# Softmax attention with a rational feed-forward part on one core: seven-token key descriptors, four-token value descriptors, score tiles by parity, scalars loaded later

## The chip, the cores and the metric

The kernel runs on one core of one Trainium2 chip. The metric is the device time of one execution in microseconds (us), the median over several executions. Every ratio compares with the kernel before on the same chip, in alternating rounds. All executions that this study quotes were classed as fast by the measuring program, so no slow run is mixed in.

The engines are TensorE (PE in the listings; PEld is its weight loading), VectorE (DVE), ScalarE (ACT), GpSimd (POOL) and SyncE (SP). GpSimd issues most loads from DRAM into SBUF, the on-chip memory. PSUM is the small memory into which TensorE writes its results. "L540" is a line of the kernel. The same statement has another line number in the kernel before and after, for example the first linear layer is L539 before and L540 after. The "ramp" is the first part of an execution, up to about 43 us, in which TensorE still waits for data and for other engines.

## The reference

There are 8 batches, 12 heads, 448 tokens and 64 numbers a head. The attention has one more term in its denominator. Its result goes through a linear layer (768 to 2048), a rational function of each element, and a second linear layer (2048 to 768).

```python
scores = scale * np.matmul(q, k.transpose(0, 1, 3, 2))
m = np.max(scores, axis=-1, keepdims=True)
e = np.exp(scores - m)
attn = e / (np.sum(e, axis=-1, keepdims=True) + np.exp(-m) + 1e-09)
x = np.matmul(attn, v)                    # then (batch*tokens, heads*64)
h = x @ w_in
P = a[0] + a[1]*h + a[2]*h**2 + a[3]*h**3
Q = 1.0 + abs(b[0])*abs(h) + abs(b[1])*h**2
out = (P / (Q + 1e-06)) @ w_out
```

The exponential may be taken without the maximum, since e / (sum of e + exp(-m)) is exp(score) / (sum of exp(score) + 1). That is what the kernel does.

## The kernel before

The kernel is written as steps with an estimated duration, an engine and what they depend on. A small planner walks over them when the program is built and fixes the **order** of the instructions on each engine. On the chip each engine runs its instructions in that order and waits for its operands. The planner takes written landing times of the loads, a price for a change of TensorE's tiling mode (`switch`), a further reluctance to change it, and a patience:

```python
    def order(self, switch, reluctance, patience, calm):
        ...
                for eng in cost:
                    t = max(self.free[eng], r)
                    k = key
                    if eng == "PE" and m != mode:
                        k += reluctance[self.free["PE"] > calm]
                    ahead[eng].append((t, k, s))
        ...
    plan.order(0.095, (0.05, 0.8), 1e-09, 25)
```

A head has 448 tokens, so each of 64 partitions holds seven consecutive tokens. The kernel before loads them as three, three and one. A descriptor is one such run, 768 bytes in DRAM for three tokens and 256 for one. (The loads narrow to 16 bits on the way, and the trace counts half of these bytes.) NS is 3, NT is 7, and a "quad" is one of the three groups of four heads.

```python
    def three(src, b, half):
        return src[b].rearrange("h (p j) d -> p h (j d)", j=NT)[
            :, :, NS * half * D:NS * (half + 1) * D]

    def load_rest(src, b, dsts, eng=nc.gpsimd):
        of = src[b].rearrange("h (p j) d -> p h j d", j=NT)
        for half, dst in enumerate(dsts):
            eng.dma_start(out=dst, in_=of[:, H // 2 * half:H // 2 * (half + 1), NT - 1, :])

    def load_k(b, part):
        ...
        if part < 3:
            for half in range(2):
                nc.gpsimd.dma_start(
                    out=k4[rows(half), 4 * part * w:4 * (part + 1) * w].rearrange(
                        "p (t x) -> p t x", x=w),
                    in_=of_quad(three(k, b, half), part))
        ...
        if part >= 3:
            load_rest(k, b, [...])
```

The first batches are then worked on as follows. Keys and queries are turned by TensorE (`tk`, `tq`). A score tile (`sps`) is four 64x64 matmuls. ScalarE takes its exponential (`e`, 128x896). TensorE forms the denominators (`den`, 16 matmuls) and the products with the values (`u`, two times 16). ScalarE makes the reciprocal of the denominator with a logarithm and an exponential (`rden`), and VectorE multiplies (`xt`). When all six parts of `xt` of a batch and a quarter of w_in are there, the first linear layer (`hp`, six matmuls a step) can run.

```python
        nc.scalar.activation(out=e[:, :, 0:n], in_=sps[:, :, 0:n], func=AF.Exp, scale=scale)
...
    def inverse(b, z, qd, step, eng):
        if eng == "ACT" and step == 0:
            nc.scalar.activation(out=r, in_=dens.pop((b, z, qd))[:, 0:w],
                                 func=AF.Ln, bias=one_c)
        elif eng == "ACT":
            nc.scalar.activation(out=r, in_=r, func=AF.Exp, scale=-1.0)
...
    def gemm1(b, z, fcs):
        ...
                nc.tensor.matmul(
                    out=hp[:, n * w:(n + 1) * w],
                    lhsT=w_in_sb[:, c, fc * 128:(fc + 1) * 128],
                    rhs=xt[:, c, queries(b, z)], start=(c == 0), stop=(c == NDC - 1),
                )
```

Nine matmuls on zeros (`busy_work(9)`, tile `idle`) stand at the head of TensorE's work, while the first data are on their way.

## Time and profile before

| what | value |
|---|---|
| time, three runs | 427.45 us median (427.42 to 428.1) |
| span of the profiled run | 426.0 us |
| TensorE busy | 414.5 us |
| first matmul of the first layer | 31.69 us |
| 25th matmul of the first layer, after which TensorE is nearly full | 42.56 us |

The profile's page begins with the busy time of each engine and its share of the span. Further down it lists the DMA queues: packets, megabytes, and the time of those packets as a share of all 16 DMA engines.

```profile
PE 414.5 (97%) x3693; PEld 208.6 (49%) x3693; DVE 332.0 (78%) x493; ACT 309.1 (73%) x361; POOL 113.4 (27%) x176
...
q0 software_dynamic: 55936, 22.50, 44.3%
```

The list of TensorE's waits has these lines (who waited, for what, us in total, times, longest).

```profile
PE sps L460 <- ACT e L472: 2.1, 4, 1.0
PE hp L539 <- DVE xt L524: 1.3, 1, 1.3
...
PE hp L539 <- DMA w_in_sb<-in_moe_w_in_dram: 0.6, 1, 0.6
```

TensorE waits for w_in, at 31.69 us, for 0.6 us. It waits 1.3 us at 42.56 us for a product of VectorE.

### The profile page before, as it was taken

To read this page: it belongs to the slowest core of one execution; us is meant where nothing else is said; L and a number is where in the kernel's file an instruction comes from. 1 tells how busy PE (TensorE), PEld (TensorE's weight loads), DVE (VectorE), ACT (ScalarE), POOL (GpSimd) and SP (SyncE) were. 2 spreads that over 40 slices of the span, in tenths; PEclk is the share of its full clock that TensorE was granted. 3 is DMA by queue.
4 is the path that set the end of the run, shared out by engine and by line. 5 is a ranking of instruction groups with operands and counts; after the bars stand their busy time and mean duration, and the time that the engine had idled before them with its cause. 6 is when DMAs were issued, how large, how long until landed. Compare 5 with 4: busy or idle time off the path is not lost.

```text
span 426.0 us, 8968 instructions
## 1 busy us (share of the span) xinstructions
PE 414.5 (97%) x3693; PEld 208.6 (49%) x3693; DVE 332.0 (78%) x493; ACT 309.1 (73%) x361; POOL 113.4 (27%) x176
## 2 busy tenths in 40 slices
PE   7798999999999999999999999999999999999996
PEld 3443444444554455544554455444455545556664
DVE  4446899999959995999729994139999799899721
ACT  5898887998828993498946997699998396465300
POOL 8875405542720801540008001020002000004100
PEclk9999999999999999999999999999999999999999
DMA  9999999999799999990299814970001102002223
GB/s 140 171 157 197 166 207 155 157 196 209 127 188 213 112 150 195 141 159 2 51 209 128 100 57 96 177 103 2 2 1 57 37 2 57 18 2 75 75 74 75
DMA packets 116025, 47.28 MB, mean 111 GB/s; under 512 B 90256, under 2 KB 115984, under 8 KB 115984
## 3 DMA queue, kind: packets, MB, share of 16 engines
q0 software_dynamic: 55936, 22.50, 44.3%
q1 hardware_dynamic: 59824, 24.06, 25.2%
q8 instruction: 29, 0.48, 0.5%
q10 hardware_dynamic: 224, 0.15, 0.1%
q14 instruction: 12, 0.10, 0.1%
HBM read 45.62 MB, written 11.01 MB: 133 GB/s over the span
## 4 chain that ended last, share of the span: by engine, by line
PE 76%; ACT 8%; DVE 6%; POOL 3%; DMA 3%; issue 1%; POOLq 0%; ACTq 0%
PE op L634 31%; PE hp L539 29%; PE sps L460 7%; PE u L480 6%; ACT e L472 4%; PE den L480 3%; ACT c L593 2%; DMA w_in_sb<-in_moe_w_in_dram 2%; DVE c L581 1%; DMA q<-in_q_dram 1%; POOL k L193 1%; DVE g L591 1%; DVE w L586 1%; DVE xt L524 1%; ACT g L136 1%
## 5 line engine op out<-in xcount | busy, mean ns | idle before, releaser
L539 PE MATMUL hp<-xt,w_in_sb 128*128 128x448 f16 x768 | 154.4, 353 | 1.8 <-DVE xt L524 1.3
L472 ACT ACTIVATE e<-sps 128x896 f16<-128x896 f32 x168 | 146.3, 927 | 9.1 <-PE sps L460 6.9
L634 PE MATMUL op<-w_out_sb,g 128*128 128x384 f16 x768 | 130.4, 326 | 0.1
L539 PEld LDWEIGHTS <-w_in_sb 128*128 128x128 f16 x768 | 71.6, 98 | 76.6 <-issue 13.3
L634 PEld LDWEIGHTS <-g 128*128 128x128 f16 x768 | 73.3, 98 | 54.7 <-issue 7.7
L604 POOL COPY gx<-g 128x256 f16<-128x256 f16 x32 | 23.0, 740 | 216.0 <-DVE g L591 110.2
L586 DVE TENSOR_TENSOR w<-w,g 128x1792 f16<-128x1792 f16 (+1 forms) x66 | 69.7, 1056 | 0.3
L593 ACT ACTIVATE c<-c,oneeps_c 128x1792 f16<-128x1792 f16 (+1 forms) x33 | 57.8, 1751 | 12.9 <-DVE c L581 12.9
L138 DVE CAST g<-hp 128x448 f16<-128x448 f32 x78 | 48.1, 618 | 15.7 <-PE hp L539 15.3
L460 PE MATMUL sps<-qT,kT 64*64 64x448 f16 x672 | 53.5, 365 | 3.1 <-ACT e L472 2.1
L136 ACT ACTIVATE g<-hp 128x448 f16<-128x448 f32 x50 | 27.2, 546 | 38.8 <-PE hp L539 38.7
L595 ACT ACTIVATE c<-c 128x1792 f16<-128x1792 f16 (+1 forms) x33 | 54.8, 1660 | 0.2
L524 DVE TENSOR_TENSOR xt<-u,rden 128x448 f16<-128x448 f32 x48 | 27.9, 615 | 30.6 <-ACT rden L504 29.8
L588 DVE TENSOR_SCALAR w<-w,abc 128x1792 f16<-128x1792 f16 (+1 forms) x66 | 44.8, 679 | 0.4
L136 ACT ACTIVATE osb<-op 128x384 f32<-128x384 f32 (+1 forms) x25 | 12.2, 489 | 42.8 <-DVE osb L138 23.1
L480 PE MATMUL u<-e,v 128*32 128x448 f16 x768 | 40.7, 353 | 0.0
L138 DVE COPY osb<-op 128x384 f32<-128x384 f32 (+2 forms) x33 | 17.8, 539 | 26.0 <-PE op L634 25.9
L591 DVE TENSOR_TENSOR g<-w,c 128x1792 f16<-128x1792 f16 (+1 forms) x33 | 34.8, 1054 | 1.1 <-ACT c L595 0.7
L581 DVE TENSOR_TENSOR c<-c,w 128x1792 f16<-128x1792 f16 (+1 forms) x33 | 34.8, 1054 | 0.3
L460 PEld LDWEIGHTS <-kT 64*64 64x64 f16 x672 | 15.4, 104 | 38.1 <-issue 35.8
L480 PEld LDWEIGHTS <-v 128*32 128x32 f16 x768 | 20.4, 97 | 15.6 <-issue 0.6
L583 DVE TENSOR_SCALAR w<-g,abc 128x1792 f16<-128x1792 f16 (+1 forms) x33 | 24.2, 734 | 0.4
(49 smaller groups left out, 266.4 us busy)
## 6 DMA issues: line engine op xcount, KB each, us to landing
q<-in_q_dram POOLq DMA_DIRECT2D x23, 224.0 KB, 6.0
v<-in_v_dram POOLq DMA_DIRECT2D x14, 288.0 KB, 5.6
k<-in_k_dram POOLq DMA_DIRECT2D x12, 288.0 KB, 6.8
w_in_sb<-in_moe_w_in_dram POOLq DMA_DIRECT2D x16, 192.0 KB, 7.8
w_out_sb<-in_moe_w_out_dram POOLq DMA_DIRECT2D x4, 768.0 KB, 9.3
out_dram<-osb SPq DMA_DIRECT2D x16, 168.0 KB, 2.3
out_dram<-osb SPq DMA_DIRECT2D x16, 144.0 KB, 1.9
out_dram<-osb SPq DMA_DIRECT2D x16, 120.0 KB, 1.8
```

What stands on the lines that cost most here:

```text
L136: nc.scalar.activation(out=out, in_=src, func=AF.Copy)
L138: nc.vector.tensor_copy(out=out, in_=src)
L460: nc.tensor.matmul(out=sps[rows(c), bank, m * w:(m + 1) * w], lhsT=kT[rows(half), key:key + 64], rhs=qT[rows(half), o:o + w], start=True, ...
L472: nc.scalar.activation(out=e[:, :, 0:n], in_=sps[:, :, 0:n], func=AF.Exp, scale=scale)
L480: nc.tensor.matmul(out=dst[32 * t:32 * t + 32], lhsT=lhs(t, n), rhs=ets[b, z, qd, i][:, bank, m * w:(m + 1) * w], start=(n == 0), stop=(n ...
L539: nc.tensor.matmul(out=hp[:, n * w:(n + 1) * w], lhsT=w_in_sb[:, c, fc * 128:(fc + 1) * 128], rhs=xt[:, c, queries(b, z)], start=(c == 0), ...
L581: nc.vector.tensor_tensor(out=c, in0=c, in1=m, op=ALU.mult)
L586: nc.vector.tensor_tensor(out=m, in0=m, in1=h, op=ALU.mult)
L588: nc.vector.tensor_scalar(out=m, in0=m, scalar1=a1 if step == 5 else a0, scalar2=None, op0=ALU.add)
L593: nc.scalar.activation(out=c, in_=c, func=AF.Ln, bias=oneeps_c)
L595: nc.scalar.activation(out=c, in_=c, func=AF.Exp, scale=-1.0)
L634: nc.tensor.matmul(out=op[:, 0:wide_of(nh)], lhsT=lhs(fc), rhs=w_out_sb[:, fc, columns(nh)], start=(fc == 0), stop=(fc == NFC - 1),)
```

## The change

The change has six parts, in one diff.

1. Keys come with all **seven tokens in one descriptor**, values with four (or three), so there are fewer descriptors and fewer load instructions.
2. The score tiles pair tokens s and s + 4 and are sorted by head parity (from batch 2 on by the parity of head, quad and token together).
3. The early key load takes whole runs of seven. Keys of the first quad are therefore narrowed to 16 bits and turned in pieces.
4. The two small loads of the scalars a and b are issued later.
5. The order of the loads changes. Three quarters of w_in now stand ahead of the values of batch 1.
6. The written landing times, the planner's parameters and the start keys are new, and there are 18 small filler steps of one matmul on zeros. In the second linear layer the steps of batch 0 are sorted, and output copies of batch 2 no longer go to ScalarE.

```diff
-    def three(src, b, half): ...
-    def load_rest(src, b, dsts, eng=nc.gpsimd): ...
+    def keys_of(b, half, qd=None):
+        some = k[b, H // 2 * half:H // 2 * (half + 1)].rearrange("h (p j) d -> p h (j d)", j=NT)
+        return some if qd is None else some.rearrange("p (t g) x -> g p t x", g=NQ)[qd]
 ...
+        for half in range(2):
+            to = loaded[b, "k"][rows(half)].rearrange("p (h x) -> p h x", x=NT * D)
+            if part < 3:
+                to = to.rearrange("p (t g) x -> g p t x", g=NQ)[part]
+            nc.gpsimd.dma_start(out=to, in_=keys_of(b, half, part if part < 3 else None))
 ...
+        for above, half, n0, n1, heads in classes():          # values: four or three tokens
+            first = above + n0
+            nc.gpsimd.dma_start(
+                out=v4[rows(half), heads].rearrange("p h s d -> p h (s d)")[
+                    :, :, first * D:(first + n1 - n0) * D],
+                in_=of_half(v, b, half, n0, n1, heads))
 ...
-    nc.sync.dma_start(out=abc, in_=moe_a.unsqueeze(0).to_broadcast([128, 4]))
-    nc.sync.dma_start(out=bbc, in_=moe_b.unsqueeze(0).to_broadcast([128, 2]))
+    def load_scalars():
+        for dst, src in ((abc, moe_a), (bbc, moe_b)):
+            nc.vector.memset(dst, 0.0)
+            nc.sync.dma_start(out=dst, in_=src.unsqueeze(0).to_broadcast(dst.shape))
 ...
+        ('k0', 2), ('q0', 1), ('k0', 1), ('q0', 2), ('v0', 4), ('k1', 4),     # first loads
+        ('q1', 0), ('q1', 2), ('q1', 1), ('w', 0), ('w', 1), ('w', 2), ('v1', 4),
 ...
+    for n in range(1, 19):
+        add("warm", ("warm", n), 1000, {"PE": (0.22, 0.22)}, lambda: busy_work(1),
+            deps=[("s", 0, 0, 0, 0)], takes=[("gen", ("warm", n))], mode="full")
 ...
-        for t, eng, name, fn in plan.order(0.095, (0.05, 0.8), 1e-09, 25):
+        for t, eng, name, fn in plan.order(0.095, (0.2, 1.0), 0.3, 60):
```

## The prediction

> **What bounds the kernel now.** I read first the busy time of the engines by stretch (columns: stretch, its length, busy us and instructions of PE, weight loads, DVE, ACT and POOL, the granted clock, DMA share, GB/s).
>
> ```profile
> 0.00:5.00 5.00, 3.80 (x9) 1.19 (x9) 1.86 (x13) 1.28 (x1) 3.82 (x11) 1.00 0.60 122
> 5.00:31.70 26.70, 22.36 (x422) 11.88 (x422) 12.05 (x30) 23.22 (x32) 22.38 (x39) 1.00 1.36 162
> 31.70:43.00 11.30, 9.93 (x107) 4.22 (x108) 6.82 (x11) 9.43 (x12) 6.69 (x11) 1.00 1.41 197
> 43.00:110.00 67.00, 66.69 (x609) 31.25 (x608) 66.03 (x95) 59.20 (x66) 24.32 (x31) 1.00 1.15 177
> ...
> 422.00:426.00 4.00, 0.00 (x0) 0.00 (x0) 0.27 (x1) 0.33 (x1) 0.00 (x0) 0.89 0.25 56
> ```
>
> TensorE is full from 43 us to 422 us: 0.31 us are missing in the first 67 us of it and similarly little later. Of the 11.5 us without TensorE work, 1.2 lie before its first instruction, 4.0 after its last, 4.34 between 5 and 31.7 us (26.70 less 22.36), 1.37 between 31.7 and 43. The last two, 5.7 us or 1.3% of the time, are all that earlier data can give back. Anything more has to come from less TensorE work.
>
> Next the chain that ended last, in order of time, as far as the first matmul of the first linear layer (start, us, what).
>
> ```profile
> 3.92 2.46 POOL k L193 x4
> ...
> 7.18 6.03 DMA q<-in_q_dram
> ...
> 18.30 1.32 POOL k L181 x2
> 19.62 0.71 POOL q L163
> 20.33 1.23 POOL v L211 x2
> 21.56 0.91 POOL w_in_sb L380 x2
> ...
> 23.19 8.37 DMA w_in_sb<-in_moe_w_in_dram
> ...
> 31.69 1.30 PE hp L539 x6
> ```
>
> Until 31.69 us the chain is GpSimd issuing loads one after the other and the first quarter of w_in landing behind them. After that TensorE has big independent matmuls to put between the attention steps, so the start of the first linear layer is the moment at which TensorE becomes full. Last, ScalarE in the same stage (timeline; start, us, instructions, idle before).
>
> ```profile
> 15.89 2.53 ACT L472 ACTIVATE e<-sps 128x896 f16<-128x896 f32 x3
> 20.00 3.35 ACT L472 ACTIVATE e<-sps 128x896 f16<-128x896 f32 x4 [1.57 <-PE u L480]
> ...
> 29.31 0.64 ACT L501 ACTIVATE rden<-den,one_c 128x448 f32<-128x448 f32 x1
> 29.98 0.58 ACT L504 ACTIVATE rden<-rden 128x448 f32<-128x448 f32 x1
> ```
>
> ScalarE is the second limit of the ramp. Its exponentials begin at 7.30 us, take 0.83 us each when they follow one another (five in 4.15), and batch 0 needs 21 of them and three reciprocals of 0.54 + 0.58. The last reciprocal ends at 30.56, the last attention product on DVE near 31.7. So in the kernel before w_in and the attention of batch 0 are ready at practically the same time, and **both** must move for a gain.
>
> **What the skill says.** The page "DMA: Bandwidth & Descriptors", section "Why small descriptors are slow (HBM only)", gives each packet a fixed cost beside its bytes. The trace agrees in direction. From 0 to 28 us, 11365 packets carried 4.62 MB (407 B each); from 40 to 50 us, 2649 packets carried 1.96 MB (740 B each). With 16 engines busy for about 26 and 10 us, a packet took 36.6 and 60.4 ns. A straight line through these two (my estimate from two points) is 7.5 ns a packet and 0.0715 ns a byte. The page "TensorEngine Tiling (Array Packing)", section "Key Properties", says that a change of tiling mode drains TensorE. Here 6 matmuls of the first layer take 1.24 us alone and 18.16/16 = 1.135 us inside a run of 96; 16 of the second take 2.71 alone and 2.60 in a run. So a change of mode costs some **0.1 us**. The page "TensorE: Matmul & The Clock Gate", section "What's actually happening", says that an idle window of about 3.4 us halves the clock. Here the longest wait of TensorE in the ramp is 1.3 us and the granted clock is 1.00 throughout: there is no clock to win.
>
> **The change, part by part.**
>
> *Fewer descriptors and fewer issues.* Keys of a batch go from 1536 runs of three tokens and 768 of one to 768 of seven. By the line above that is 1536 x (7.5 + 27.5) + 768 x (7.5 + 9.2) = 66.6 engine-us before and 768 x (7.5 + 64.1) = 55.0 after, or 4.2 and 3.4 us on 16 engines. Values go from 2304 runs to 1536 of four or three tokens: 4.2 to 3.8 us. Two key batches (a third of one comes by the early loads anyway) and one value batch lie ahead of w_in: about 1.8 us less DMA. GpSimd issues 28 loads before the first of w_in now, and 16 afterwards: 12 x 0.66 us = 7.9 us less issuing, in a stage where it is 22.38/26.70 busy. Issuing and transfer overlap, so the sum doesn't count. Taking 2 to 4 us together, w_in lands at **27.5 to 29.5** instead of 31.55 us. The landing times written into the changed kernel say 28.7 for it against 32.0 in the old one; they order instructions only, but point the same way.
>
> *ScalarE's part of the ramp.* One key load per half, with tokens 0 and 4 narrowed first, should bring the first exponential from 7.3 to about 6.6 us; query and key loads of quads 1 and 2 come earlier, values all at once near 17 us. Then 6.6 + 21 x 0.83 + 3 x 1.12 = 27.4 is the earliest end of the last reciprocal, with two products of 0.58 us 28.6. Allowing for half of the old idle time, the first layer starts at about **29 us** instead of 31.69. The same attention work lies before it: 22.36 us of TensorE, less two score tiles of batch 1 (0.6) and with 0.3 more for the key transposes, which for the first quad go in halves (98 instead of 84, at 0.044 us). So idle time from 5 to 29 us is 24.0 - 22.1 = 1.9 instead of 4.34: **-2.4 us**.
>
> *The gap at 42.6 us* (1.29 us, matmuls waiting for a product that gives back their PSUM buffer) belongs to the old order of work. I give the new order an even chance: **-0.7**.
>
> *Score tiles by parity.* Number, shape and pairing in the array stay: 168 tiles of four 64x64 matmuls, seven to a head quad. No cost: **0**.
>
> *The new order.* The timeline of TensorE shows 212 changes of mode, 166 of them after 43 us; there, 18 stretches of scores are a single tile and 58 a pair. Greater reluctance to change (0.2 and 1.0 instead of 0.05 and 0.8) should pair some of them. Each pairing saves two changes, 0.2 us; four pairings give **-0.8**.
>
> *Scalars later, filler matmuls.* The two scalar loads leave the head of the SyncE queue; their transfers are 1.1% of DMA there: 0. Up to 18 fillers of 0.22 us run only where the plan sees TensorE idle, but each is a change to full mode and takes a PSUM buffer: **+0.2**, though the profile will count up to 4 us of them as busy.
>
> *Stages after 110 us.* DMA is below full there and TensorE full, so cheaper key and value loads buy nothing.
>
> **The rivals.** (1) *A new wait for values of batch 1.* The changed load order puts three quarters of w_in ahead of them, yet the written landing times still have them at 31.8 us, before the second quarter of w_in. Three quarters at 786 KB and 196 GB/s are 4 us each, so after 27.7 + 8.0 + 3.9 they land near 39.6. If TensorE reaches those products in order at 35 to 36 us it stalls for up to 4 us, and scores behind it stall too. For it speaks the inconsistency, against it that someone tuning on the chip would have seen it. A chance of one in four of 2.5 us: **+0.6** in the mean; if it comes, the time is 426.5 to 428. (2) *ScalarE stays the bound of the ramp.* Then w_in lands early for nothing, and only the switches and the earlier start pay: 426 to 427. For it speaks 23.22 of 26.70 us busy; against it the 1.57 us wait, which comes from waiting on values in order. (3) *The new order of the whole kernel also makes TensorE's work shorter*, by pairing nearly all scores and joining runs of the layers: 30 changes fewer are another 3 us, so 421 to 422. Nothing in the profile before speaks for so many.
>
> **Range and chances.** -2.4 - 0.7 - 0.8 + 0.2 + 0.6 = -3.1 us, and I take 0.2 back for instructions that the new plan misplaces elsewhere: 427.45 - 2.9, **about 424.5 us**. Rivals 1 and 2 set the upper end, 428.0, rival 3 and the whole 5.7 us of gaps the lower, 421.0. Faster by over 2% needs under 419.1 us, more than all idle time of the ramp: 4%. Slower by over 2%, above 436 us, would need several stalls of 4 us: 2%. Within 2%: 94%.
>
> **What would show it.** Right: w_in lands at 27.5 to 29.5 us, the first matmul of the first layer starts near 29, idle time of TensorE from 5 to 31.7 us apart from fillers falls below 2.5 us, software queue packets fall from 55936 by 8 x 2304 = 18432 less the part now loaded early, to about 37500, and the score group keeps its 168 x 4 matmuls at some 365 ns. The switches part is shown by under 210 changes of mode, fillers aside. Wrong: a wait of TensorE for values at 35 to 40 us (rival 1); a first exponential not before 7 us or a last reciprocal of batch 0 after 29.5 (rival 2); gaps of TensorE after 43 us of over 1 us in sum; or a clock below 1.00 in the ramp. Should the time fall by over 6 us, my claim that TensorE's work stays the same is what failed.

## The result, and the profile after

| | before | after |
|---|---|---|
| median of the rounds | 427.77 us (427.42 to 429.41, 4 runs) | 429.96 us (429.57 to 430.16, 4 runs) |
| span of the profiled run | 426.0 us | 428.4 us |
| software queue packets | 55936 | 37376 |
| TensorE busy | 414.5 us | 420.9 us |

The ratio is 1.0043, with a 95% interval of 1.0019 to 1.0066. A ratio here is the mean time of one kernel's runs over that of the other's of the same rounds, so it is not quite the ratio of the quoted medians. The result lies within 2%, as predicted, but about 2 us on the slow side. That is outside the predicted range, whose upper end was 428.0 us. A second series of the same changed kernel on another chip gave 1.0022 (0.9995 to 1.0049).

The page of the changed kernel answers the two lines shown of before.

```profile
PE 420.9 (98%) x3725; PEld 212.0 (49%) x3725; DVE 330.8 (77%) x489; ACT 313.4 (73%) x366; POOL 95.8 (22%) x152
...
q0 software_dynamic: 37376, 22.47, 37.9%
```

The descriptors did what they were meant to do: a third fewer packets for the same bytes, 17.6 us less GpSimd work. TensorE's busy time has **grown** by 6.4 us, but not through more useful work. The 18 fillers take 4.63 us of it by TensorE's timeline (0.39 + 0.61 + 0.61 in the ramp and 3.02 at the end). A stretch at half the TensorE clock, shown below, adds about 2.4 us; this is worked out from the same groups at full speed in other runs. What is left, 6.4 - 4.6 - 2.4, is -0.6 us. A higher busy share is no gain here.

The busy time by stage, with the columns of the prediction's windows. The last line is the stage in which the loads of the ramp overlap most.

```profile
5.00:31.70 26.70, 23.17 (x382) 12.15 (x384) 9.79 (x25) 22.04 (x29) 16.43 (x29) 0.87 1.31 192
31.70:43.00 11.30, 11.22 (x140) 4.77 (x132) 6.66 (x13) 8.87 (x13) 7.63 (x13) 1.00 1.37 199
43.00:110.00 67.00, 65.92 (x594) 31.13 (x591) 66.69 (x97) 58.73 (x66) 22.35 (x32) 1.00 1.14 176
...
20.00:31.70 11.70, 10.37 (x191) 5.51 (x186) 4.78 (x10) 10.84 (x15) 6.50 (x11) 1.00 1.25 198
```

The kernel before moved less in the last of these:

```profile
20.00:31.70 11.70, 10.68 (x211) 5.44 (x204) 6.05 (x13) 11.15 (x15) 8.81 (x16) 1.00 1.26 157
```

So the loads run at 198 instead of 157 GB/s, and the idle time of TensorE from 31.7 to 43 us is gone (11.22 of 11.30, before 9.93). But from 43 to 110 us TensorE now misses 1.08 us instead of 0.31, and in the ramp its granted clock is 0.87 in the mean.

The chain that ended last, up to the first layer (start, us, what):

```profile
3.74 6.17 DMA q<-in_q_dram
...
9.96 0.96 PE tq L285 x13
10.91 0.55 PE sps L458 x4
...
11.48 0.93 ACT e L470
...
26.35 2.54 ACT e L470 x3
...
30.43 0.87 PE den L478 x16
31.30 1.51 PE u L478 x32
32.82 0.50 PE sps L458 x8
...
33.66 2.38 PE hp L540 x12
```

The chain before ran over GpSimd's issues and the landing of w_in. Now it follows GpSimd and a load only until the queries land, at 9.91 us. From 10 us to the first layer the chain alternates between exponentials on ScalarE and small groups on TensorE, and w_in doesn't occur. ScalarE's timeline has the same moments as in the prediction (start, us, instructions, idle before):

```profile
11.48 2.54 ACT L470 ACTIVATE e<-sps 128x896 f16<-128x896 f32 x3 [1.54 <-PE sps L458]
...
32.02 0.58 ACT L502 ACTIVATE rden<-rden 128x448 f32<-128x448 f32 x1
```

The last reciprocal of batch 0 ends at 32.60 us, not at 27.4. The 1.57 us wait for values at 20 us is gone, but a wait of 1.54 us for a score tile stands at 11.48 us in its place. From TensorE's list of waits, the lines that take the place of those shown of before (its waits for ScalarE are unchanged, 2.0 us in all):

```profile
PE tq L285 <- DMA q<-in_q_dram: 1.2, 1, 1.2
...
PE hp L540 <- DVE xt L525: 0.3, 1, 0.3
```

**A marker that means the same in both kernels.** In both, 24 matmuls of the first layer come early, mixed with attention of batch 1. The start of the 25th is the moment after which TensorE is nearly full; I call it the resumption. Here it is in TensorE's timeline, first before, then after.

```profile
42.56 3.57 PE L539 MATMUL hp<-xt,w_in_sb 128*128 128x448 f16 x18 [1.29 <-DVE xt L524]
```

```profile
43.08 1.31 PE L540 MATMUL hp<-xt,w_in_sb 128*128 128x448 f16 x6
44.32 0.58 PE L285 MATMUL tq<-ident,q 112*64 112x112 f16 x16
```

With it the 2.40 us between the two profiled spans (428.4 - 426.0) can be split:

| part | before | after | difference |
|---|---|---|---|
| start to resumption | 42.56 | 43.08 | +0.52 |
| resumption to TensorE's last output matmul | 379.32 | 380.93 | +1.61 |
| from there to the end | 4.12 | 4.39 | +0.27 |

In the middle part TensorE idles 1.31 us (380.93 - 379.62) instead of 0.53 (379.32 - 378.79), which is 0.78. The windows, first before, then after:

```profile
42.56:421.88 379.32, 378.79 (x3160) 191.53 (x3160) 311.05 (x440) 275.30 (x318) 80.93 (x118) 1.00 0.64 105
```

```profile
43.08:424.01 380.93, 379.62 (x3191) 192.69 (x3188) 311.80 (x438) 280.46 (x324) 67.87 (x100) 1.00 0.59 102
```

The last 22 transposes of batch 1, the sixteen `tq` shown and six `tk` at 47.41 us, stand behind the resumption, about 0.8 us. In the kernel before all of them stand in front of it. This is a plain count from two traces. A second profile of each kernel, from two other chips (after_again and before_again below), gives +0.1, +1.35 and +0.25 for the same three parts. The middle part is steady: 379.3 to 379.7 us in the four profiles of the kernel before and its edits, 380.7 to 381.2 us in nine of the changed kernel and its edits (after, after_again, fill_wait, q_first, no_tail, w_late, hold_clock, scal_early, load_best), with and without a half-speed stretch in the ramp. So most of the loss lies **after** the ramp.

### The profile page after: what moved, and what is told of

Its sections match the earlier page's. It is cut to its first block, busy times and chain, and to the rows that moved or that the text cites. A ratio compares the mean times of both kernels' runs of the same rounds, so it can differ in the third digit from the quotient of the medians.

```text
span 428.4 us, 8992 instructions
## 1 busy us (share of the span) xinstructions
PE 420.9 (98%) x3725; PEld 212.0 (49%) x3725; DVE 330.8 (77%) x489; ACT 313.4 (73%) x366; POOL 95.8 (22%) x152
## 3 DMA queue, kind: packets, MB, share of 16 engines
q0 software_dynamic: 37376, 22.47, 37.9%
## 4 chain that ended last, share of the span: by engine, by line
PE 82%; ACT 8%; DVE 7%; DMA 1%; issue 1%; POOL 0%; POOLq 0%; DVEq 0%
PE op L635 33%; PE hp L540 29%; PE sps L458 8%; PE u L478 7%; ACT e L470 5%; PE den L478 4%; DMA q<-in_q_dram 1%; DVE w L587 1%; DVE g L138 1%; ACT c L594 1%; DVE w L589 1%; DVE g L592 1%; DVE c L582 1%; PE idle L335 1%; PE tk L320 1%
## 5 line engine op out<-in xcount | busy, mean ns | idle before, releaser
L540 PE MATMUL hp<-xt,w_in_sb 128*128 128x448 f16 x768 | 152.5, 353 | 0.3 <-DVE xt L525 0.3
L605 POOL COPY gx<-g 128x256 f16<-128x256 f16 x32 | 25.7, 830 | 212.7 <-issue 76.3
L136 ACT ACTIVATE g<-hp 128x448 f16<-128x448 f32 x62 | 34.3, 553 | 34.2 <-PE hp L540 34.2
L138 DVE CAST g<-hp 128x448 f16<-128x448 f32 x66 | 40.9, 620 | 19.1 <-PE hp L540 19.0
L138 DVE COPY osb<-op 128x384 f32<-128x384 f32 (+2 forms) x39 | 21.2, 544 | 30.8 <-PE op L635 30.7
L136 ACT ACTIVATE osb<-op 128x384 f32<-128x384 f32 (+1 forms) x19 | 9.3, 488 | 33.8 <-DVE osb L138 23.4
L578 DVE TENSOR_SCALAR c<-w,babs 128x1792 f16<-128x1792 f16 (+1 forms) x33 | 24.6, 745 | 0.3
```

The costliest lines, as they stand in the source:

```text
L136: nc.scalar.activation(out=out, in_=src, func=AF.Copy)
L138: nc.vector.tensor_copy(out=out, in_=src)
L540: nc.tensor.matmul(out=hp[:, n * w:(n + 1) * w], lhsT=w_in_sb[:, c, fc * 128:(fc + 1) * 128], rhs=xt[:, c, queries(b, z)], start=(c == 0), ...
```

## The experiments

My first theory was the wait and the clock at 9 to 16 us. TensorE waits 1.19 us for queries of quad 1, which the plan thinks are there at 9.2 us. After it, every TensorE group takes nearly twice as long until about 16.3 us. The rivals: the ramp is bound by ScalarE and by the way it alternates with TensorE; the filler matmuls cost time; the new order costs time later. All outputs are right.

### fill_wait: keep TensorE busy over the wait

```diff
-        ... lambda: busy_work(1),
+        ... lambda n=n: busy_work(6 if n == 1 else 1),
```

> Only edit: the filler before the transposes of query quad 1 is 6 matmuls instead of 1, so that TensorE has work in the 1.19 us in which it waits for that load (8.8 to 9.95 us); every other instruction keeps its order and the wait itself stays. Theory A (the wait lets the granted clock fall to half from about 9.3 to 16.2 us, and the slow clock is most of the loss): the granted clock from 5 to 31.7 us is 1.00 instead of 0.87, the first matmul of the first linear layer starts near 31.5 instead of 33.60 us, and the median falls by 1.5 to 2.5 us, to 427.5 to 428.5. Theory B (the order of work around the wait starves ScalarE, and the clock is incidental because TensorE has slack there): the clock may recover, but the first layer still starts after 33 us and the time stays within 0.5 us of 429.96.

Measured: 429.88 us against 427.89, ratio 1.0046 (1.002 to 1.0073). In the profiled run the clock stayed at full speed and the first layer started at 31.96 us, 1.6 us earlier than in the first profile of the changed kernel. The median didn't follow: the profiled run was the fastest of the six (428.57 us).

### q_first: queries of quad 1 loaded before keys of quad 2

```diff
-        ('k0', 2), ('q0', 1), ('k0', 1),
+        ('q0', 1), ('k0', 1), ('k0', 2),
```

> Only edit: the load of query quad 1 is issued before the key loads of quads 2 and 1 (order q1, k1, k2 instead of k2, q1, k1); TensorE, DVE, ScalarE keep their order instruction by instruction. Its data should land near 8 us instead of 9.9. Theory A: the wait of 1.19 us is gone or below 0.3, the clock stays at 1.00, the time falls to 427 to 428.3. Theory B: ScalarE is fed 1 to 1.5 us earlier at 10 us, time falls by about 1 us even if the clock should fall. Both expect a gain; it tells them apart only together with fill_wait: under A the two gain about the same, under B this one gains and fill_wait does not.

Measured: 428.5 us, ratio 1.0014 (0.9989 to 1.0038). The wait for queries is gone. TensorE waits 1.13 us for ScalarE's narrowing of the keys instead, and the profile still shows half-speed groups, from 7.82 to 11.4 us.

### late_q: tell the plan that these queries land later

```diff
-        ('ld', 'q', 0, 1): 9.2,
+        ('ld', 'q', 0, 1): 10.4,
```

> Only edit: the landing time written for query quad 1 is 10.4 us instead of 9.2, so the plan puts one more score tile of quad 0 (and a filler on each side of it) before the transposes of quad 1, instead of after them. No load changes. Theory A: the wait for the load shrinks to under 0.4 us since useful work is done meanwhile, the clock stays at 1.00, and the time falls to 427 to 428.5. Theory B: ScalarE gets its tile at about 9 us and its idle time of 1.54 us at 10 to 11.5 us shrinks to under 0.7; the time falls by 0.5 to 1 us whatever the clock does. If the clock still falls with the wait gone, it is not the wait that makes it fall.

Measured: 428.9 us, ratio 1.0015 (0.9988 to 1.0041). The wait is gone, the half-speed stretch stays (8.2 to 14.7 us), and the first layer starts at 33.87 us. The profiled run was the slowest of its six (429.62 us) and that of fill_wait the fastest, so their first layers don't speak for the medians. q_first and late_q look up to 1 us better than the unchanged changed kernel elsewhere (1.0043 and 1.0022), but that kernel was not run in these rounds. This gain is therefore not shown.

### no_tail: four fillers instead of eighteen

```diff
-    for n in range(1, 19):
+    for n in range(1, 5):
```

> Only edit: 4 single fillers are planned instead of 18. In the changed kernel 14 of the 18 are never placed in idle time and run at the very end, 3.0 us after the last output matmul. Theory C (the tail costs time): the last store has been issued before the fillers end, so 0.3 us of the span goes, from 428.4 to about 428.1, and the clock still falls. If the tail were hidden behind the stores: no change. Under A and B the tail is a side matter: at most 0.5 us.

Measured: 429.06 us, ratio 1.0029 (1.0004 to 1.0054). Only four of the 18 fillers found a place. The other 14 stood at the end of TensorE's order and ran after its last real matmul. The end of the chain, first in the changed kernel, then here:

```profile
424.02 3.02 PE idle L335 x14
```

```profile
422.68 0.36 DVE osb L138
...
423.11 0.33 ACT osb L136
```

Without them the end follows the last output copy again, as in the kernel before. From the last output matmul to the end it is 4.06 us here, 4.08 and 4.10 in the two later runs without them, and 4.32 to 4.40 in the profiles with them. By the profiles the fillers at the end cost **0.27 us** (4.39 - 4.12); the medians can't resolve so little.

### after_again: the changed kernel once more, as a control

No edit.

> The changed kernel itself, unedited, as the control on the chip of these runs, since four runs are few beside the spread that showed up (426.5 to 429.6 us for the kernel before). Expected: 1.003 to 1.005 of the kernel before, the granted clock below 0.997 in most runs, every run at a lower clock slower by about 1.2 us for each 0.004 of clock (one stretch of about 3.4 us at half clock).

Measured: 429.44 us against 428.16, ratio 1.0022 (0.9995 to 1.0049). The wait for queries was only 0.16 us in this profile, and yet the groups around it run at half speed:

```profile
9.62 0.96 PE L285 MATMUL tq<-ident,q 112*64 112x112 f16 x16 [0.16 <-DMA q<-in_q_dram]
```

```profile
9.00:12.00 3.00, 2.84 (x26) 1.10 (x26) 0.62 (x1) 2.18 (x4) 2.20 (x6) 1.00 1.32 180
```

The second line is a window of the same run, with the clock third from the end. The granted clock says 1.00. Sixteen of these matmuls take 0.58 us at full speed, so a clock record of 1.00 doesn't rule out a slow stretch. Here it lasts from the first matmul, at 1.2 us, to about 13.5 us. The expected 1.2 us for each 0.004 of recorded clock did not show: one run at 1.00 took 429.24 us, three at 0.992 took 429.56 on average.

### w_late: w_in some seven microseconds later

```diff
-        ('w', 0), ('w', 1), ('w', 2), ('v1', 4), ('q2', 0), ('q2', 1),
+        ('v1', 4), ('q2', 0), ('q2', 1), ('w', 0), ('w', 1), ('w', 2),
```

> Only edit: the values of batch 1 and two query quads of batch 2 are loaded before the first three quarters of w_in instead of after them, so the first quarter lands some 5 us later than its 25.5 us, near 30.5. All other engines keep their order. Theory B (ScalarE and the attention of batch 0 set the start of the first linear layer, and the 6 us by which w_in lands earlier are unused): the start of the layer stays within 0.5 us of 33.6 us minus whatever the clock gives, and the time within 0.7 us of the control. Rival (the load of w_in is still what the start waits for, directly or through the queue): the layer starts later by 2 us or more, the time rises by 1.5 to 4 us.

Measured: 429.69 us, ratio 1.0031 (1.0002 to 1.0059), with the control of the same chip at 429.44. GpSimd issues the first part of w_in at 21.91 us here and at 14.32 in the changed kernel. The first layer of this run in TensorE's timeline:

```profile
32.98 2.44 PE L540 MATMUL hp<-xt,w_in_sb 128*128 128x448 f16 x12
```

The first layer doesn't wait for what was issued 7.6 us later: no wait stands in brackets, and the chain of waits of this run has no w_in either. So the earliness of w_in, on which the larger part of the predicted gain was built, is **not used**. It is used up here, though: the fourth piece of the first quarter was issued at 24.88 us, and the shortest time from issue to landing in this run is 7.3 us, so it landed at 32.2 us or later.

### act_more: two microseconds more on ScalarE

```diff
+        if (b, qd, i) == (0, 1, 3):
+            for _ in range(5):
+                nc.scalar.activation(out=spare, in_=zeros[:, 0:256], func=AF.Copy)
         e = att.tile([128, 2, S], F16, tag="e", name="e", bufs=12)
```

> Only edit: five spare copies of 128x256 on ScalarE, some 0.35 us each and 1.5 to 1.8 us in sum, put ahead of one exponential of batch 0 (quad 1, tile 3, near 20 us). No other engine gets an instruction more. Theory B (ScalarE is the bound of the ramp): the last reciprocal of batch 0, the start of the first layer and the end of the run all move later by about the same 1.5 us. Rival (TensorE, by its slow clock, is the bound, and ScalarE has slack): the added copies fill ScalarE's waits, and the time rises by less than 0.5 us.

Measured: 431.78 us, ratio 1.0077 (1.0047 to 1.0108), 2.34 us over the control. The five added instructions (duration in ns: least, median, most; first and last start):

```profile
L472 ACT ACTIVATE spare<-zeros x5: 416/417/423, 19.4 to 21.2; 128x256 f16<-128x256 f16 x5
```

Five times 417 ns is 2.08 us. The first layer, in TensorE's timeline:

```profile
36.12 2.44 PE L544 MATMUL hp<-xt,w_in_sb 128*128 128x448 f16 x12
```

That is 2.52 us later than in the first profile of the changed kernel (the half-speed stretch lies at the same place in both), and the median rises by 2.34 us. A part of this may come with the clock, since three of the six runs recorded 0.988. Between the three at 0.992 and the control's three at 0.992 it is 1.50 us (431.06 against 429.56). ScalarE's work in the ramp is on the path: 2.08 us of it cost 1.5 to 2.3 us.

### hold_clock: full TensorE speed from 7 us on

```diff
     (fill_wait's edit, and in transpose_k:)
+        if up == 1:
+            busy_work(5)
```

> Edits: six filler matmuls instead of one before the transposes of query quad 1, and five more before the transposes of the second half of the first key quad, where TensorE waits 0.4 to 1.1 us for ScalarE. Theory A (the slow clock is most of the loss): the clock is 1.00 in nearly all runs, and the time falls to that of the few runs of the earlier variants at 1.00, 427.5 us or 1.000 of the kernel before. Theory B: the clock holds but the time falls by at most 1 us, because the fillers themselves delay TensorE when loads come early, and ScalarE still begins its exponentials after 7 us.

Measured: 429.34 us, ratio 1.0025 (0.9994 to 1.0056), with the control at 429.44. All six runs recorded a clock of 1.00, and in the profiled one the groups agree:

```profile
10.49 0.58 PE L285 MATMUL tq<-ident,q 112*64 112x112 f16 x16
```

Full speed buys 0.1 us, which these rounds cannot tell from nothing. The edit has a cost of its own: five fillers stand ahead of the key transposes, and the first exponential comes at 7.67 us instead of 7.10. So a gain of some tenths may be hidden. But the kernel before, in its five runs of these rounds that recorded 0.998 or more, took 427.84 us on average, and these six took 429.52. At full recorded clock on both sides the loss is still 1.7 us. The clock theory (theory A of the first expectations) is **not upheld**.

### recip_one, recip_dve and recip_best: reciprocals moved to VectorE

```diff
-    ON_DVE = []
+    ON_DVE = [(0, 0, 0)]                  # recip_one
+    ON_DVE = [(0, 0, 0), (0, 0, 1)]       # recip_dve
     # recip_best: recip_one with the edits of q_first and no_tail
```

> Only edit: the reciprocal of head quad 0 of batch 0 is formed on DVE (add and reciprocal, about 0.6 + 3.8 us there, where DVE is idle) instead of by two activations of 0.54 and 0.58 us on ScalarE; the exponentials keep their order, TensorE's order changes by a few score tiles near 28 us. Theory B (ScalarE is the bound of the ramp, shown by more work there): less work there must help as more work hurt. The last reciprocal of batch 0 and the start of the first layer come 0.8 to 1.2 us earlier than in a run of the changed kernel with the same stretch of slow matmuls, and the median falls by 0.7 to 1.2 us. If instead TensorE limits (score tiles not ready), ScalarE only waits longer and the time falls by less than 0.4 us.

> As recip_one, but for head quads 0 and 1 of batch 0. Takes 2.3 us from ScalarE; DVE's reciprocal of 3.8 us stands in order before copies of transposed keys and queries and may delay score tiles of batch 1. Theory B: the first layer starts 1.5 to 2 us earlier; the time falls by 1 to 2 us unless the delayed copies open a new wait later. If it gains less than recip_one, DVE has become the bound there.

> The version that the runs point to: recip_one, query quad 1 loaded before the keys of quads 1 and 2 (q_first) and only 4 fillers (no_tail). Sum of the single gains: 0.9 + 0.9 + 0.3 = some 2 us below the changed kernel, near 427.4 us, or 0.997 to 1.000 of the kernel before. If it stays above 1.002, the gains of q_first and recip_one are the same microsecond (ScalarE's wait near 10 us).

Measured, all on one chip: recip_one 430.01 us, ratio 1.0043 (1.0019 to 1.0068). recip_dve 432.07, ratio 1.0107 (1.008 to 1.0134). recip_best 429.0, ratio 1.0031 (1.0007 to 1.0054). ScalarE is relieved of one reciprocal of some 1.1 us in recip_one. Its timeline shows what it does with it, and VectorE's shows the price:

```profile
19.12 4.16 ACT L470 ACTIVATE e<-sps 128x896 f16<-128x896 f32 x5 [1.10 <-PE sps L458]
```

```profile
15.83 2.95 DVE L507 RECIPROCAL rden<-rden 128x448 f32<-128x448 f32 x1
```

ScalarE now **waits** 1.10 us for a score tile, where it waited 0.35 us in the changed kernel. TensorE's order puts 32 products (`u`) ahead of that tile, and it can't be overtaken. So ScalarE is not a bound by its busy time alone. It and TensorE hand work to each other in a fixed order, and taking work from one leaves the other's turn in place. The last reciprocal of batch 0 ends at 31.09 us, 0.55 us earlier than in after_again's profile, whose half-speed stretch ends at the same 13.5 us; no gain reached the median. In the profile of recip_dve TensorE waits 2.78 us, at 65.79 us, for queries of batch 2 that are turned by DMA. But that run took 434.89 us and the other five 431.64 to 432.83, so this wait may belong to that run alone; where the median of recip_dve loses stays open.

### scal_early: the scalars loaded at the start again

```diff
-    add("babs", ("abc",), 2, {"DVE": (0.15, 0.25)}, load_scalars, deps=[("ex", 0, 0, 1, 0)])
+    load_scalars()          # directly after its definition
```

> Undoes one part: the six scalars of the rational part are loaded at the start again, from the SyncE queue behind the early query and key loads, instead of after an exponential near 16 us. Expected: within 0.3 us of the changed kernel (two issues of 0.4 to 0.6 us on an idle queue, 224 small packets). If late scalars were a part of the loss, it would be faster by more than 0.5 us; if they were needed for the early key loads, slower by more than 0.5.

Measured: 430.08 us, ratio 1.0055 (1.0032 to 1.0078). Undoing the part doesn't make the kernel faster. There is no unchanged control on that chip, so whether late scalars are a small gain stays open; they are not the cause of the loss.

### before_again: the kernel before against itself

No edit of the kernel before.

> The kernel before, unedited, as one of the kernels under test: a second profile of it. Its first profile had no slow stretch in the ramp, read from the durations of the matmuls (16 query transposes 0.58 us at full speed, 0.96 at half), and started the first layer at 31.69 us. If slow stretches come to this kernel as often as to the changed one, and cost it as much, they do not explain the difference of the two; expected then: a slow stretch of 3.4 us or more before 17 us and a first layer 0.7 us or more later. If its ramp has no slow stretch again, they may.

Measured: 427.31 us against 427.82, ratio 0.9986 (0.9962 to 1.001). The method gives about 1 for equal kernels. One seventh of a per cent, 0.6 us, came by chance here; differences of that size below show nothing.

### k1_first: the early keys before the early queries

```diff
+        for half, eng in enumerate((nc.scalar, nc.sync)):   # keys, moved up
+            ...
         nc.sync.dma_start(out=wide["q"]..., in_=by_quad(q, 0, 0)[:, 0:n])
-        for half, eng in enumerate((nc.scalar, nc.sync)):
-            ...
```

> Only edit: on the SyncE queue the early load of the second half of the first key quad is issued ahead of the early query load instead of behind it; computing engines keep their order. In the profiles of the changed kernel and its variants TensorE waited 0.4 to 1.7 us at 6.5 to 8.1 us for ScalarE to narrow these keys, which landed at 6.1 to 7.1 us. Theory D (the two big early key loads, 224 KB each instead of four of 96, feed the ramp too late): the keys land near 5.3 us, the wait is below 0.3 us, the first layer starts about 0.8 us earlier than in a run with the same slow stretch, and the median falls by 0.6 to 1 us against the changed kernel (1.000 to 1.002 of the kernel before). Rival: the query now comes later and stops the very first transposes at 5.15 us, no gain.

Measured: 429.88 us, ratio 1.004 (1.002 to 1.0061). The wait has changed hands. It is the longest of TensorE's in this run, and ScalarE's first exponential comes at 9.24 us, 2.1 us later than in the changed kernel:

```profile
PE tq L285 <- DVE q L138: 2.2, 1, 2.2
```

The first layer starts at 34.04 us, 0.44 us later than in the first profile of the changed kernel and 1.41 us later than in that of after_again. So a part of such an early delay is absorbed by the waits that follow. How much can't be said from these three, since the half-speed stretch lies elsewhere in each (7.4 to 13.9 us here).

### old_params and load_best: the planner's old parameters; the load edits together

```diff
-        ... plan.order(0.095, (0.2, 1.0), 0.3, 60):
+        ... plan.order(0.095, (0.05, 0.8), 1e-09, 25):     # old_params
     # load_best: the edits of k1_first, q_first and no_tail
```

> Undoes one part: the plan's reluctance, patience and calm are those of the kernel before (0.05 and 0.8, 1e-9, 25 us instead of 0.2 and 1.0, 0.3, 60), the loads and keys of work stay. If the new values are part of the loss (they pair score tiles in the ramp, and ScalarE waits 0.35 to 0.58 us behind each long run of TensorE), the time falls by more than 0.5 us and ScalarE's waits before 33 us sum to under 2 us. If they were a gain that something else ate: time rises by 0.5 us or more and changes of mode go up from 213.

> Three edits of loads and tail together: k1_first, q_first (query quad 1 ahead of the key loads of quads 1 and 2) and 4 fillers instead of 18; order of computing work as in the changed kernel but for one swap near 28 us. Theory D says that the ramp's loads are what can be mended: 0.8 + 0.9 + 0.3 us, so near 427.5 us and 0.998 to 1.000 of the kernel before. If it stays at 1.002 or more, the loads of the ramp are not what holds the changed kernel back.

Measured, on the chip of k1_first: old_params 429.05 us, ratio 1.0017 (0.9996 to 1.0038). load_best 429.4, ratio 1.003 (1.001 to 1.0049). The new parameters bring no gain. The old ones look 0.4 to 0.8 us better than their two neighbours, within overlapping intervals.

### before_cold and before_values: the same stage in the kernel before

```diff
-    ... lambda: busy_work(9),
+    ... lambda: busy_work(3),             # before_cold: a cold start
-        ('q1', 0), ('v0', 0), ('k1', 0), ('q0', 2), ('k1', 2), ('v0', 3), ('k1', 1),
+        ('v0', 0), ('v0', 3), ('q0', 2), ('q1', 0), ('k1', 0), ('k1', 2), ('k1', 1),   # before_values
```

> An edit of the kernel before: its first burst of 9 filler matmuls is 3, so TensorE works at half speed in the ramp (some 3.4 to 10 us of it, read from the durations of matmuls); order and loads stay. This puts the suspected cost of the changed kernel, the slow stretch, into the kernel before without its loads. Theory A in its modest form (the slow stretch costs the ramp 1.2 to 1.7 us, the rest of the loss lies elsewhere): the first layer starts 1 to 1.7 us after 31.6 us and the median rises by 1 to 1.7 us to some 1.003 of the kernel before. If the ramp has slack for it, as the control and hold_clock of the changed kernel (0.1 us apart) may say: under 0.5 us.

> An edit of the kernel before, aimed at beating both: in its load order the values of quad 0 and the last tokens of all values, and query quad 2, come before the query and key loads of batch 1. Compute order stays. The profile of the kernel before shows ScalarE idle for 1.57 us near 18.4 us behind products that wait for values in order; the changed kernel has not this wait, with its values loaded at once. Expected: that wait falls below 0.3 us; w_in lands as before at 31.5 us, so the first layer can gain at most 0.2 us at once, but batch 1 is further on: 0 to 1 us less, 0.998 to 1.000. If the first layer starts later than 32.5 us, keys of batch 1 now come too late.

Measured: before_cold 427.99 us against 428.46, ratio 0.999 (0.9976 to 1.0004). before_values 427.85, ratio 0.9985 (0.9969 to 1.0). before_values looks 0.6 us faster, but its interval touches 1, and the unedited kernel differed from itself by as much (before_again). TensorE's timeline of before_cold:

```profile
9.48 0.59 PE L460 MATMUL sps<-qT,kT 64*64 64x448 f16 x4
...
32.14 1.31 PE L539 MATMUL hp<-xt,w_in_sb 128*128 128x448 f16 x6
...
41.95 3.58 PE L539 MATMUL hp<-xt,w_in_sb 128*128 128x448 f16 x18
```

At 9.48 us a score tile takes 0.59 us, at 12.93 us 0.38: TensorE is slow until about 12 us. The first layer starts 0.45 us later than in the profile of the kernel before, and the resumption comes 0.6 us **earlier**, without the wait in brackets. In before_values it is 0.7 us later and 0.36 us earlier:

```profile
32.39 1.31 PE L539 MATMUL hp<-xt,w_in_sb 128*128 128x448 f16 x6
...
42.20 3.58 PE L539 MATMUL hp<-xt,w_in_sb 128*128 128x448 f16 x18
```

So in the kernel before, the start of the first layer had slack behind it, the 1.29 us wait at 42.56 us. The slack varies: in the profile of before_again that wait is 0.68 us (first layer 31.46, resumption 42.02), and against that profile the resumption of before_values is 0.18 us later.

## Why the prediction was right or wrong

**Fewer descriptors and issues: right.** Packets fell to 37376 (said: about 37500). GpSimd was busy 16.43 us from 5 to 31.7 us instead of 22.38. The first quarter of w_in was issued from 14.3 to 18.3 us instead of 21.5 to 23.75. By the 7.3 to 10.8 us from issue to landing it was there near 25.5 us, even before the predicted 27.5.

**ScalarE's part of the ramp: this is the step that failed.** It read "6.6 + 21 x 0.83 + 3 x 1.12 = 27.4 is the earliest end of the last reciprocal", and from it a first layer at about 29 us. The last reciprocal ended at 32.60 and the first layer began at 33.60 us. The terms, as measured in the changed kernel:

| term | said | first profile | fill_wait, full speed from about 6 us |
|---|---|---|---|
| first exponential | 6.6 us | 7.10 us | 7.26 us |
| exponentials before the last reciprocal | 21 | 22 | 22 |
| ScalarE's waits between them | none in the bound, half the old idle time of TensorE later | 3.55 us (0.20, 1.54, 0.48, 0.54, 0.35, 0.44) | 1.78 us (0.20, 0.79, 0.35, 0.44) |
| end of the last reciprocal | 27.4 us | 32.60 us | 30.97 us |

The waits are the largest. In the kernel before they were 1.77 us (0.20, 1.57), and 22 exponentials stood there too. The argument took away the 1.57 and put nothing in its place. Without the later half-speed stretch the changed kernel waits as long as the kernel before, only elsewhere; in the first profile, with the stretch, it waits 1.77 us longer. Yet every score tile waits for a free buffer from ScalarE, and every exponential for a tile, in an order fixed beforehand. recip_one showed this: of 1.1 us of work taken from ScalarE, 0.75 us returned at one place (a wait of 1.10 us instead of 0.35). act_more showed the other half: 2.08 us of work added came out as 1.5 to 2.34 us in the time. Rival 2, "ScalarE stays the bound of the ramp", is what came, in a stronger form. The prediction gave it 426 to 427 us, because it still credited the switches and an earlier start.

**The marker was wrong too.** The prediction said that the start of the first linear layer "is the moment at which TensorE becomes full". before_cold and before_values contradict that. In the kernel before, the first layer could slip by 0.7 us (32.39 in before_values against 31.69) while the last output matmul ended at 421.90 us against 421.88, because of the wait at 42.56 us. So the steps of -2.4 and -0.7 us were not two gains. They were one stretch of slack counted in two places. The gap at 42.6 us did close (0.08 us of idle time is left from 31.7 to 43), since what came before it was 1.9 us later in that profile.

**The switches: wrong, by the whole 0.8 us.** TensorE's timeline counts 213 changes of mode after and 212 before, 167 and 166 of them after 43 us. Against the kernel before, no more scores were paired. Greater reluctance did have an effect: counted the same way, old_params has 223 changes, 172 after 43 us. So it saved some ten, which the rest of the change had added, and old_params was no slower for them (429.05 us). A gain of 0.1 us for each change saved doesn't show in the time.

**Fillers: the right sign and size, for another reason.** +0.2 us was predicted for changes of mode in the ramp. 0.27 us was measured, at the end of the kernel, from the 14 that found no place (no_tail).

**The rest after the resumption: not predicted.** The text took "TensorE's work stays the same" and allowed 0.2 us for misplaced instructions. From the resumption to the last matmul it is 1.61 us more: 0.78 us of idle time, and transposes of batch 1 that moved behind it. Gaps of over 1 us after 43 us were among the prediction's signs of being wrong, and they came (1.08 us up to 110 us). The two largest waits are for ScalarE and for a product:

```profile
78.54 0.38 PE L458 MATMUL sps<-qT,kT 64*64 64x448 f16 x4 [0.56 <-ACT e L470]
...
90.14 1.29 PE L540 MATMUL hp<-xt,w_in_sb 128*128 128x448 f16 x6 [0.28 <-DVE xt L525]
```

I argue from the two traces that the new order causes them; no run took out these two waits alone.

**Scores by parity at no cost: right.** 168 tiles of four matmuls at 370 ns a matmul, 365 before; the median is 373 ns in both, and the mean of the changed kernel contains the half-speed stretch. **Rival 1, a wait for values of batch 1: refuted.** TensorE waits for no values at 35 to 40 us. **Rival 3, shorter TensorE work by pairing: refuted** with the count of changes.

**The clock.** "A clock below 1.00 in the ramp" was named as a sign of error, and it came: 0.87 from 5 to 31.7 us. But hold_clock removed it for 0.1 us and still took 1.7 us more than the kernel before at full clock, and the kernel before bears a slow start without loss (before_cold). In several series the runs with a lower recorded clock are the slower ones: in before_again 428.36 us on average at 0.996 and 427.15 at 1.00. That is a correlation only, and the control of the changed kernel doesn't show it (429.24 us at 1.00, 429.56 at 0.992). Where the slow stretch lies may still matter, since in the first profile it lies at 9 to 16 us and the resumption is at 43.08, in after_again at 4.6 to 13.5 us and 42.12. This stays open.

**The balance.** Predicted for everything up to the resumption was -3.1 us (-2.4 - 0.7), and +0.5 came. For the rest of the sum +0.2 was predicted (-0.8 + 0.2 + 0.6 + 0.2), and +1.9 came, all of it after the resumption. Shown by experiment are that the early w_in is unused, that ScalarE's work is on the path, and the 0.27 us of the fillers. About 1.6 us, the largest part of the loss, is located in the traces after the resumption, but its causes are not separated: no run restored the old start keys, landing times, key transposes or steps of the second layer. Of the planner's part only the parameters were undone. No version of the changed kernel beat the kernel before.

## What to carry to other kernels

Before crediting an earlier load, list what else the first consumer needs, and ask whether the wait that it removes is followed by another one that would have absorbed the delay anyway: two waits in a row on the same engine are one piece of slack. Where two engines pass tiles to each other in an order fixed beforehand, the sum of one engine's busy time is no bound; walk the hand-overs, or test with a little added work (it shows at once whether the engine is on the path) and a little removed work (it shows whether the other engine lets it through). Filler work needs a place to go: what the planner can't place lands at the end and is paid in full or in part.

## What the Trainium skill lacked or had wrong

- "TensorE: Matmul & The Clock Gate", section "What's actually happening": the page has the clock halve after an idle window of about 3.4 us and recover after one busy window of that length. In the first profile of the changed kernel it halved near 9.4 us, where TensorE's longest wait was 1.19 us, and stayed so to about 16.3 us. In after_again TensorE has no wait longer than 0.16 us between 1.2 and 13.5 us and still ran at half speed for all of it. These runs don't show what rule held instead, and the page's other sections were not held against these traces.
- The same page, section "Seeing it yourself", warns that the clock's trace events are unreliable. These runs agree and give a size: a recorded clock of 1.00 from 9 to 12 us, while 16 transposes took 0.96 us instead of 0.58.
- "TensorEngine Tiling (Array Packing)", section "Key Properties": a change of mode drains TensorE, but there is no figure. By the working in the prediction it is an estimated 0.1 us here (1.24 against 1.135 us for six matmuls of the first layer); ten changes fewer than in old_params did not make the kernel faster, so the figure is not confirmed by a time.
